# A spectral block on one core: stage two regrouped onto halves of the TensorE array

## The chip, the core and the metric

The kernel runs on one core of one Trainium2 chip. The metric is the device time of one execution in microseconds, as the median of several runs. The profile is of one execution; its times are microseconds from the start of the span unless marked ns. PE is TensorE, the matrix engine, and PEld its weight loads; DVE is VectorE, ACT ScalarE, POOL GpSimd, SP SyncE, which issues the DMAs here. L492 is line 492 of the kernel.

## The reference: what is computed

A block on 2048 rows of 512 values, in fp32: a modulation vector from `c`, a layer norm, a two-dimensional FFT filter, a gated residual, a second norm, a dense layer with Mish, and a second gated residual.

```python
mod = (_silu(c) @ w_mod).reshape(c.shape[0], 6, 1, -1)
sa, ca, ga, sb, cb, gb = (mod[:, 0], mod[:, 1], mod[:, 2], mod[:, 3], mod[:, 4], mod[:, 5])
h = _layernorm(x, axis=-1) * (1 + ca) + sa
x = x + ga * irfft2(rfft2(h) * (w_r + 1j * w_i), s=(S, D))
h = _layernorm(x, axis=-1) * (1 + cb) + sb
x = x + gb * (mish(h @ w1 + b1) @ w2)
```

The filter is the part that matters here. A transform over 2048 rows is split into one of 128 and one of 16, a transform over 512 values into one of 128 and one of 4.

## The kernel before

The kernel has four stages that follow one another on TensorE.

Stage one (to about 50 us) normalises the input and does the long parts of both transforms. It leaves `a_sb`: for each of 64 columns q a tile of 128 partitions (the row frequency within 128) by 128 numbers, 16 row remainders by 8 (four value remainders, real and imaginary).

Stage two (`p2_...`, about 50 to 99.5 us) finishes the forward transform over the 16 x 8 numbers of a column, multiplies by the filter, and starts the way back. It goes over 17 groups of columns: column 0 alone (the "zero group", with its own functions `z_...`, since it also holds the values that a real transform folds away), columns 1 to 3, and then fours. A group takes five steps:

- `p2_in`: a transpose of each column on PE (L471), one copy out of PSUM by ACT (L474), and `p2_shift`, a small sum on POOL that adds the norm's shift to one element of each column (L482);
- `p2_mul`: for each column one fp32 matmul with the column as stationary operand and the constants `kf` moving, 128 x 128 (L492). The result has the row frequency on partitions;
- `p2_prod`: two DVE products of 512 with the filter's real and imaginary part (L508), then a difference and a sum of 256 each (L513, L514) on POOL, or the difference on DVE in the first and last groups;
- `p2_back`: a second transpose of each column on PE (L525) and a copy by ACT (L528);
- `p2_out`: for each column one fp32 matmul with the column stationary and `kv` moving (L538). `store_d` copies the result out of PSUM on ACT with the two operations of L391 and L392, for each of the two halves `dd[0]` and `dd[1]`.

The order is written out by hand (`manual_schedule`). The first eight groups are brought in ahead (`LEAD`), then each step s of the loop issues, in this order, products of group s, matmuls of group s + 1, transposes of group s + 3, a step of the modulation, second transposes of group s - 2 and the way back of group s - 3. PSUM has eight banks; each kind of step has two of its own (tags A to D). SBUF buffers come in rings of two by tag.

Beside the groups the same loop computes the four parts of the modulation that later stages need: 16 weight tiles of 256 KB, fetched by SP through a ring of four (`mod_fetch`, L551), each one DVE step (`mod_late`: L115, L117, or L120 with a read of the sum). The gate of the first residual is spread over partitions by a matmul with ones and multiplied into `kiv` (`mod_gate`, L563 and L564), that of the second by `apply_gate` (L568, L569) at the end. The filter comes in 16 pieces of 256 KB, `wqa` in stage one and `wqb` at the start of stage two, in the space that stage one's input ring leaves. `kc`, two transfers of 1 MB for stage three, is issued at step 9.

Stage three (from 99.5) ends the inverse transform (L676, L677, L686), adds the residual and prepares the weights of the dense layers; its first matmul needs `dd[0]` of all columns. Stage four (from about 143) is the dense layers in three-term split precision, which take the rest.

Of the kernel before, what the change touches and what calls it, by code (L numbers as in the profile page):

```python
# [12 lines left out]
P = 128  # L13
# [18 lines left out]
def tile_spectral_block(ctx: ExitStack, tc: tile.TileContext, x_d, w1_d, b1_d, w2_d,  # L32
# [68 lines left out]
    wqa = pw.tile([P, 8, 2, 64, 4], F32, name="wqa")  # L101
# [5 lines left out]
    kv = pw.tile([P, 512], F32, name="kv")  # L107
# [83 lines left out]
    def load_rest():  # L191
        nc.sync.dma_start(kf, kf_d)
        nc.sync.dma_start(wz, wz_d)
        for i in range(8):
            nc.sync.dma_start(wqa[:, i], wq_d[i])
            if i == 2:
# [189 lines left out]
    def store_d(ps, q0, nq):  # L386
        src = ps[:, 0:nq * 128].rearrange("p (q a c) -> p a c q", q=nq, c=2)
        for i in range(2):
            dst = dd[i].rearrange("p n d c q -> p (n d) c q")
            s = src[:, 32 * i:32 * i + 32]  # L390
            nc.scalar.copy(dst[:, :, 0:2, q0:q0 + nq], s)  # L391
            nc.scalar.mul(dst[:, :, 2, q0:q0 + nq], s[:, :, 0, :], -1.0)  # L392

    groups = [(0, 1), (1, 3)] + [(q0, 4) for q0 in range(4, NQ, 4)]

    seq = [1, 2, 3, 4, 0] + list(range(5, len(groups)))
    early = [big.tile([P, 4, 512], F32, name=f"early{i}", tag=t) for i, t in enumerate(("cr", "ci"))]

    def zbuf(g):
        i = seq.index(g)  # L400
        return early[i // 4][:, i % 4] if i < 8 else buf("h")
# [13 lines left out]
    def z_in():  # L415
        ps = bank("A")
        nc.tensor.transpose(ps[:, 0:P], a_sb[:, 0, :, :].rearrange("p n e -> p (n e)"), ident)
        z = zbuf(0)
        turned(z, ps[:, 0:P])
        nc.gpsimd.tensor_tensor(z[:, 0:1], z[:, 0:1], saz[:, 0:1], op=ALU.add)  # L420
        st["z", 0] = z

    def z_mul():
        z = st.pop(("z", 0))
        pb = bank("B")
        reflected(pb[:, 0:160], z, lambda i: kf[:, 128 + 160 * i:288 + 160 * i])
        st["pb", 0] = pb

    def z_prod():
        pb = st.pop(("pb", 0))  # L430
        pbv = pb[:, 0:160].rearrange("p (c j k) -> p c j k", c=2, j=5)
        pr = []
        for i in range(2):
            t = buf(("g1", "g2")[i])
            tv = t[:, 0:160].rearrange("p (c j k) -> p c j k", c=2, j=5)
            nc.vector.tensor_tensor(tv, pbv, wz[:, i].unsqueeze(1).to_broadcast([P, 2, 5, N2]), op=ALU.mult)
            pr.append(t)
        y = buf("y")
        nc.gpsimd.tensor_tensor(y[:, 0:80], pr[0][:, 0:80], pr[1][:, 80:160], op=ALU.subtract)
        nc.gpsimd.tensor_tensor(y[:, 80:160], pr[0][:, 80:160], pr[1][:, 0:80], op=ALU.add)  # L440
        nc.gpsimd.tensor_copy(y[:, 160:256].rearrange("p (i k) -> p i k", i=3),
                              y[:, P:P + 32].unsqueeze(1).to_broadcast([P, 3, 32]))
        st["y", 0] = y

    def z_back():
        y = st.pop(("y", 0))
        pc = bank("C")
        nc.tensor.transpose(pc[:, 0:P], y[:, 0:P], ident)
        nc.tensor.transpose(pc[0:96, P:2 * P], y[:, 160:256], ident)
        t1, t2 = buf("t"), buf("t")  # L450
# [7 lines left out]
    def z_out():  # L458
        t1, t2 = st.pop(("t", 0))
        pe = bank("D")  # L460
        reflected(pe[:, 0:P], t1, lambda i: kv[:, 128 + i * P:256 + i * P], [(t2[0:96, 0:P], kw)])
        store_d(pe, 0, 1)

    def p2_in(g):
        if g == 0:
            return z_in()
        q0, nq = groups[g]
        w = nq * P
        ps = bank("A")
        for i in range(nq):  # L470
            nc.tensor.transpose(ps[:, i * P:(i + 1) * P],  # L471
                                a_sb[:, q0 + i, :, :].rearrange("p n e -> p (n e)"), ident)
        z = zbuf(g)
        nc.scalar.copy(z[:, 0:w], ps[:, 0:w])  # L474
        st["z", g] = z
        if seq.index(g) >= 2:
            p2_shift(g)

    def p2_shift(g):
        q0, nq = groups[g]  # L480
        zc = st["z", g][:, 0:nq * P:P]
        nc.gpsimd.tensor_tensor(zc, zc, saz[:, q0:q0 + nq], op=ALU.add)  # L482

    def p2_mul(g):
        if g == 0:
            return z_mul()
        q0, nq = groups[g]
        w = nq * P
        z = st.pop(("z", g))
        pb = bank("B")  # L490
        for i in range(nq):
            nc.tensor.matmul(pb[:, 0:w].rearrange("p (e q) -> p e q", q=nq)[:, :, i], z[:, i * P:(i + 1) * P],  # L492
                             kf[:, 0:128], start=True, stop=True)
        st["pb", g] = pb

    def p2_prod(g):
        if g == 0:
            return z_prod()
        q0, nq = groups[g]
        w = nq * P  # L500
        pb = st.pop(("pb", g))
        pbv = pb[:, 0:w].rearrange("p (c j q) -> p c j q", q=nq, c=2)
        pr = []
        for i in range(2):
            t = buf(("g1", "g2")[i])
            tv = t[:, 0:w].rearrange("p (c j q) -> p c j q", q=nq, c=2)
            wt = (wqa, wqb)[q0 // 32][:, q0 // 4 % 8, i, :, q0 % 4:q0 % 4 + nq]
            nc.vector.tensor_tensor(tv, pbv, wt.unsqueeze(1).to_broadcast([P, 2, 64, nq]), op=ALU.mult)  # L508
            pr.append(t)
        y = buf("y")  # L510
        u = w // 2
        eng = nc.vector if g in (*seq[:3], *seq[-2:]) else nc.gpsimd
        eng.tensor_tensor(y[:, 0:u], pr[0][:, 0:u], pr[1][:, u:w], op=ALU.subtract)  # L513
        nc.gpsimd.tensor_tensor(y[:, u:w], pr[0][:, u:w], pr[1][:, 0:u], op=ALU.add)  # L514
        st["y", g] = y

    def p2_back(g):
        if g == 0:
            return z_back()
        q0, nq = groups[g]  # L520
        w = nq * P
        y = st.pop(("y", g))
        pc = bank("C")
        for i in range(nq):
            nc.tensor.transpose(pc[:, i * P:(i + 1) * P], y[:, 0:w].rearrange("p (e q) -> p e q", q=nq)[:, :, i],  # L525
                                ident)
        t = buf("t")
        nc.scalar.copy(t[:, 0:w], pc[:, 0:w])  # L528
        st["t", g] = t

    def p2_out(g):
        if g == 0:
            return z_out()
        q0, nq = groups[g]
        t = st.pop(("t", g))
        pd = bank("D")
        for i in range(nq):
            nc.tensor.matmul(pd[:, i * P:(i + 1) * P], t[:, i * P:(i + 1) * P], kv[:, 0:128],  # L538
                             start=True, stop=True)
        store_d(pd, q0, nq)  # L540

    late = {}
    work_mod = {s: [] for s in range(len(seq) + 4)}
    when = (3, 4, 5, 6, 6, 7, 8, 9, 9, 10, 11, 12, 12, 13, 14, 16)
    for i, s in enumerate(when):
        work_mod[s].append((i // 4, i % 4))

    def mod_fetch(s):
        for which, k in work_mod.get(s, ()):
# [11 lines left out]
    def mod_gate():  # L561
        ga = bank("A")
# [3 lines left out]
    def apply_gate():  # L566
        gb = bank("B")
# [4 lines left out]
    wqb = pw.tile([P, 8, 2, 64, 4], F32, name="wqb", tag="half")  # L572
    with tc.manual_schedule():
        for i in range(8):
            nc.sync.dma_start(wqb[:, i], wq_d[8 + i])
        for i in range(LEAD):
            p2_in(seq[i])
            if i == 1:
                for g in seq[:2]:
                    p2_shift(g)  # L580
            if i in (2, 4):
                p2_mul(seq[i // 2 - 1])
            if i == 3:
                p2_prod(seq[0])
        for s in range(len(seq) + 3):
            mod_fetch(s + 2)
            if 0 < s < len(seq):
                p2_prod(seq[s])
            if 2 <= s + 1 < len(seq):
                p2_mul(seq[s + 1])  # L590
            if LEAD <= s + 3 < len(seq):
                p2_in(seq[s + 3])
            mod_late(s)
            if 2 <= s < len(seq) + 2:
                p2_back(seq[s - 2])
            if s >= 3:
                p2_out(seq[s - 3])
            if s == 7:
                mod_gate()
            if s == 14:  # L600
                plus_one(cols[:, 1, 1, :], cols[:, 1, 1, :])
            if s == 9:
# [377 lines left out]
def _constants():  # L980
# [79 lines left out]
    kv = np.concatenate([bwd(4, backward)] + [m[:128] for m in zero], 1)  # L1060
# [6 lines left out]
def _layout(x, w_r, w_i, w_mod):  # L1067
# [12 lines left out]
    wq = wq.reshape(2, 128, 4, 16, 16, 4).transpose(4, 1, 0, 2, 3, 5).reshape(16, 128, 2, 64, 4)  # L1080
# [36 lines left out]
```

## Time and profile before

| | us |
|---|---|
| median of 3 runs | 390.17 |
| lowest and highest | 389.27, 391.98 |
| profiled execution | 389.86 |
| its span | 387.8 |
| TensorE busy | 380.7 |
| VectorE busy | 298.9 |
| ScalarE busy | 247.2 |
| GpSimd busy | 96.3 |

The time of an execution is some 2 us over its span: 389.86 beside 387.8. A busy time is a union, so overlapping instructions count once. Matmuls are pipelined: the duration that a row gives for one is its latency, and the cost of one in a row of many is the distance from start to start. An fp32 matmul stands in the trace as two weight loads and two matmul records. In a merged row of the timeline the first number is the start, the second the length of the whole row, and xN the count; what stands in square brackets is the idle time ahead of it and what ended it.

### The profile page before, as it was taken

Reading aid. Unit: us, or ns where it says so; the run is one execution under the profiler, and the core shown is the slowest. Engines: PE = TensorE matmul, PEld = TensorE weight load, DVE = VectorE, ACT = ScalarE, POOL = GpSimd, SP = SyncE. Lnnn points to the kernel's source line nnn. Section 1 sums busy time; section 2 is a strip of 40 time slices with the busy share of each in tenths; the row PEclk is TensorE's granted clock in tenths of the full one; section 3 lists DMA queues with packets and bytes.
Section 4 is the critical chain, followed back from the end, with each engine's and each line's share of the span. In section 5 each row is a group of like instructions: output and inputs, shape, how many; then the busy total and the mean of one; then the engine's idle time right before and its main releaser. Section 6 shows DMA issues by size and latency. Waiting matters only on the chain.

```text
span 387.8 us, 7373 instructions
## 1 busy us (share of the span) xinstructions
PE 380.7 (98%) x2744; PEld 353.1 (91%) x2744; DVE 298.9 (77%) x668; ACT 247.2 (64%) x545; POOL 96.3 (25%) x132
## 2 busy tenths in 40 slices
PE   8999999999999999999999999999999999999996
PEld 8899789999999998998998998999999999899984
DVE  2898879777199989897866965965966875987993
ACT  1788656678459746985755664674674675584750
POOL 0677636675067543210000000000000010017000
PEclk9999999999999999999999999999999999999999
DMA  7999995481224420200100100100100200122011
GB/s 250 380 308 348 313 341 154 122 339 41 70 83 120 132 62 28 57 1 2 56 0 3 54 2 0 57 0 2 55 2 0 76 0 2 55 70 94 3 54 54
DMA packets 21316, 36.70 MB, mean 95 GB/s; under 512 B 3841, under 2 KB 6753, under 8 KB 21025
## 3 DMA queue, kind: packets, MB, share of 16 engines
q1 hardware_dynamic: 21280, 36.24, 28.2%
q8 instruction: 21, 0.34, 0.4%
q14 instruction: 15, 0.11, 0.1%
HBM read 32.04 MB, written 4.20 MB: 93 GB/s over the span
## 4 chain that ended last, share of the span: by engine, by line
PE 84%; DVE 5%; DMA 4%; ACT 4%; issue 1%; SPq 0%; DVEq 0%; ACTq 0%
PE bank L818 24%; PE bank L765 20%; PE bank L767 10%; PE bank L492 3%; PE bank L538 3%; PE bank L686 3%; PE bank L677 3%; PE bank L676 3%; PE bank L810 2%; PE bank L830 2%; DMA modr<-scb 2%; PE bank L655 2%; PE bank L471 2%; PE bank L258 2%; PE bank L525 1%
## 5 line engine op out<-in xcount | busy, mean ns | idle before, releaser
L775 ACT ACTIVATE buf<-bank,b1n 128x256 f32<-128x256 f32 (+1 forms) x88 | 40.7, 471 | 63.9 <-PE bank L767 62.7
L776 DVE TENSOR_TENSOR buf<-buf,bank 128x256 f32<-128x256 f32 (+1 forms) x88 | 35.3, 417 | 36.4 <-ACT buf L775 36.4
L728 DVE TENSOR_TENSOR al<-buf,ah 128x512 fp32r<-128x512 f32 (+2 forms) x85 | 53.8, 658 | 0.7 <-ACT ah L727 0.7
L747 POOL TENSOR_TENSOR buf<-buf,modr 128x512 f32<-128x512 f32 (+1 forms) x3 | 3.9, 1293 | 180.5 <-DVE buf L776 144.4
L765 PE MATMUL bank<-h2o,w1h 128*128 128x512 f32 (+1 forms) x176 | 47.9, 394 | 0.0
L765 PE MATMUL bank<-h2e,w1h 128*128 128x512 f32 (+1 forms) x176 | 47.9, 394 | 0.0
L727 ACT CAST ah<-buf 128x512 fp32r<-128x512 f32 (+2 forms) x85 | 43.0, 548 | 1.2 <-DVE buf L792 1.2
L792 DVE TENSOR_TENSOR buf<-buf 128x128 f32<-128x128 f32 x148 | 39.9, 311 | 3.5 <-ACT buf L782 2.2
L782 ACT ACTIVATE buf<-buf 128x512 f32<-128x512 f32 (+1 forms) x48 | 28.6, 596 | 15.8 <-DVE buf L776 15.7
L818 PE MATMUL bank<-w2a,ah 128*128 128x256 f32 x161 | 34.6, 284 | 0.0
L765 PEld LDWEIGHTS bank<-h2o,w1h 128*128 128x128 f32 (+1 forms) x176 | 29.8, 186 | 4.6 <-DVE buf L776 0.3
L765 PEld LDWEIGHTS bank<-h2e,w1h 128*128 128x128 f32 (+1 forms) x176 | 30.0, 186 | 4.2
L818 PE MATMUL bank<-w2b,ah 128*128 128x256 f32 x147 | 31.3, 279 | 0.0
L767 PEld LDWEIGHTS bank<-h2o,w1l 128*128 128x128 f32 (+1 forms) x176 | 26.8, 185 | 4.0
L767 PEld LDWEIGHTS bank<-h2e,w1l 128*128 128x128 f32 (+1 forms) x176 | 26.7, 186 | 4.0
L767 PE MATMUL bank<-h2e,w1l 128*128 128x256 f32 (+1 forms) x176 | 27.8, 280 | 0.0
L767 PE MATMUL bank<-h2o,w1l 128*128 128x256 f32 (+1 forms) x176 | 27.8, 280 | 0.0
L818 PEld LDWEIGHTS bank<-w2a,ah 128*128 128x128 f32 x161 | 26.3, 188 | 0.0
L677 PE MATMUL bank<-kc,d 128*128 128x128 f32 x128 | 24.8, 276 | 0.0
L676 PE MATMUL bank<-kc,d 128*128 128x128 f32 x128 | 24.7, 275 | 0.0
L818 PEld LDWEIGHTS bank<-w2b,ah 128*128 128x128 f32 x147 | 24.2, 188 | 0.0
L127 DVE BATCH_NORM_STATS2 st<-x 128x6 f32<-128x512 f32 x32 | 22.0, 688 | 0.4
(224 smaller groups left out, 999.2 us busy)
## 6 DMA issues: line engine op xcount, KB each, us to landing
buf<-in_B_w_dram SPq DMA_DIRECT2D x20, 256.0 KB, 2.9
x<-in_A_x_dram SPq DMA_DIRECT2D x16, 256.0 KB, 5.1
xring<-in_x_t_dram SPq DMA_DIRECT2D x16, 256.0 KB, 5.0
wm<-in_w_mod_dram SPq DMA_DIRECT2D x16, 256.0 KB, 4.4
out_dram<-x SPq DMA_DIRECT2D x7, 512.0 KB, 2.6
mraw<-in_km_dram SPq DMA_DIRECT2D x16, 128.0 KB, 4.7
wqa<-in_w_q_dram SPq DMA_DIRECT2D x8, 256.0 KB, 4.4
wqb<-in_w_q_dram SPq DMA_DIRECT2D x8, 256.0 KB, 6.1
```

The source lines that it names most:

```text
L127: nc.vector.bn_stats(t, x[:, n, :])
L676: nc.tensor.matmul(o, dj[:, 0:128], kc[0][:, n, :], start=True, stop=False)
L677: nc.tensor.matmul(o, dj[:, 64:192], kc[1][:, n, :], start=False, stop=True)
L727: nc.scalar.copy(h, r)
L728: nc.vector.tensor_tensor(l, r, plain(h), op=ALU.subtract)
L765: nc.tensor.matmul(ps, w1h[:, k, fs], h[:, k], start=(k == 0), stop=False)
L767: nc.tensor.matmul(ps[:, 0:256], w1l[:, k, fs], h[:, k, 0], start=False, stop=(k == 3))
L775: nc.scalar.activation(o, ps[:, 256:], AF.Identity, bias=b1n[:rows, f:f + 1])
L776: nc.vector.tensor_tensor(o, o, ps[:, 0:256], op=ALU.add)
L782: nc.scalar.activation(o, o, AF.Mish)
L792: nc.vector.tensor_tensor(o, p, q, op=op)
L818: nc.tensor.matmul(o, a[p][:, e], w2[t][q][:, r], start=(own and half == 0 and t == 1 and i == 0), stop=(end and i == 2 and (n, half) != ( ...
```

## The change

Stage two goes over eight pairs of groups, eight columns each, and swaps the operands of the product by `kf`.

- `p2_in` transposes whole columns of `a_sb` as before, eight a pair into two banks, and ACT copies each bank back over the columns in `a_sb` (`zs`). One `p2_shift` covers the pair.
- `p2_mul`: `kf` is the stationary operand, 64 of its columns at a time, and the four transposed columns of a group are moving, 512 wide. The two groups of a pair (h) write to the lower and upper 64 partitions of one bank, that is they use two halves of the array's columns; c picks the real or the imaginary 64 columns of `kf`. So there are four matmuls of 512 a pair where there were eight of 128. The result has the transform's lanes on partitions, 64 of each group, real and imaginary parts in two banks.
- `p2_prod`: four DVE products of 512 and a difference and a sum of 512; the difference is on POOL, the sum on POOL, or on DVE for the last two pairs. The filter's tiles are laid out on the host to match, in eight pieces of 512 KB.
- `p2_back` is gone for all but the zero group.
- `p2_out`: for each column and each c a matmul with 64 partitions of the product as stationary operand, real and imaginary part accumulating. The two groups of a pair lie on the two halves of the array's rows and write two banks. So there are 16 matmuls of 64 x 128 by 128 a pair where there were eight of 128 x 128. `kv` holds its 64 rows twice, once for each half.
- The zero group does without its own first transpose, since column 0 is transposed with its pair, and its steps are issued between those of the pairs.
- All banks come from one ring over the eight. The last pair's second stores are on DVE.
- The fetches of the modulation have a new distribution over the pairs; the first three stand between the first and second piece of `wqb` on SP's queue. `kc` is issued in iteration 3 of eight.

```diff
-    wqa = pw.tile([P, 8, 2, 64, 4], F32, name="wqa")
+    wqa = pw.tile([P, 4, 2, 512], F32, name="wqa")
...
-    kv = pw.tile([P, 512], F32, name="kv")
+    kv = pw.tile([P, 640], F32, name="kv")
...
+    def ring():
+        return bank("ABCD"[next(count) % 4])
+
+    zs = a_sb.rearrange("p q n e -> p q (n e)")
+    lanes = 64
...
+    def p2_in(p):
+        for h in range(2):
+            ps = ring()
+            for i in range(4):
+                nc.tensor.transpose(ps[:, i * P:(i + 1) * P], zs[:, 8 * p + 4 * h + i], ident)
+            nc.scalar.copy(z_of(p, h), ps)
+
+    def z_of(p, h):
+        return zs[:, 8 * p + 4 * h:8 * p + 4 * h + 4].rearrange("p q s -> p (q s)")
+
+    def p2_shift(p):
+        zc = zs[:, 8 * p:8 * p + 8, 0]
+        nc.gpsimd.tensor_tensor(zc, zc, saz[:, 8 * p:8 * p + 8], op=ALU.add)
+
+    def p2_mul(p):
+        st["pb", p] = pbs = []
+        for c in range(2):
+            pb = ring()
+            for h in range(2):
+                nc.tensor.matmul(pb[lanes * h:lanes * h + lanes], kf[:, lanes * c:lanes * c + lanes], z_of(p, h),
+                                 start=True, stop=True)
+            pbs.append(pb)
+
+    def p2_prod(p):
+        re, im = st.pop(("pb", p))
+        wr, wi = ((wqa, wqb)[p // 4][:, p % 4, i] for i in range(2))
+        t = [buf(tag) for tag in ("y", "t", "g1", "g2")]
+        st["y", p] = t[:2]
+        nc.vector.tensor_tensor(t[0], re, wr, op=ALU.mult)
+        nc.vector.tensor_tensor(t[1], re, wi, op=ALU.mult)
+        nc.vector.tensor_tensor(t[2], im, wi, op=ALU.mult)
+        nc.gpsimd.tensor_tensor(t[0], t[0], t[2], op=ALU.subtract)
+        nc.vector.tensor_tensor(t[3], im, wr, op=ALU.mult)
+        eng = nc.vector if p >= 6 else nc.gpsimd
+        eng.tensor_tensor(t[1], t[1], t[3], op=ALU.add)
+
+    def p2_out(p):
+        y = st.pop(("y", p))
+        pd = ring(), ring()
+        for i in range(4):
+            o = slice(i * P, i * P + P)
+            for c in range(2):
+                for h in range(2):
+                    if (p, h, i) != (0, 0, 0):
+                        rs = slice(lanes * h, lanes * h + lanes)
+                        nc.tensor.matmul(pd[h][:, o], y[c][rs, o], kv[rs, c * P:c * P + P],
+                                         start=(c == 0), stop=(c == 1))
+        last = p == pairs - 1
+        for i, h in ((i, h) for i in range(2) for h in range(2)):
+            nq = 3 if (p, h) == (0, 0) else 4
+            store_d(pd[h], 8 * p + 4 * h + 4 - nq, nq, i, nc.vector if last and h else None)
...
+    work_mod = [(0, 1), (1, 2), (2, 3), (3, 2), (4, 3), (5, 3), (6, 2)]
...
+        for i in range(4):
+            nc.sync.dma_start(wqb[:, i], wq_d[4 + i])
+            if i == 0:
+                mod_fetch(0)
+                mod_fetch(1)
+        for p in range(2):
+            p2_in(p)
+            p2_shift(p)
+        for p in range(pairs):
+            p2_mul(p)
+            if p == 0:
+                z_in()
+            if p + 2 < pairs:
+                p2_in(p + 2)
+            if p:
+                p2_out(p - 1)
+            if p == 1:
+                z_mul()
+            if p == 3:
+                z_back()
+            if p == 4:
+                mod_gate()
+            p2_prod(p)
+            if p == 1:
+                z_prod()
+            if p + 2 < pairs:
+                p2_shift(p + 2)
+            mod_late(p)
+            mod_fetch(p + 2)
...
+        z_out()
+        p2_out(pairs - 1)
         apply_gate()
```

More of the change, by code (lines that the diff above doesn't have):

```diff
@@ L384, in tile_spectral_block, with store_d @@
     dd = [big.tile([P, 8, 4, 3, NQ], F32, name=f"d{i}", tag=t) for i, t in enumerate(("da", "db"))]
[L386 to L390, printed above, removed]
+    def store_d(ps, q0, nq, i, eng=None):
+        src = ps[:, (4 - nq) * P:].rearrange("p (q a c) -> p a c q", q=nq, c=2)
+        dst = dd[i].rearrange("p n d c q -> p (n d) c q")
+        s = src[:, 32 * i:32 * i + 32]
+        if eng is None:
             nc.scalar.copy(dst[:, :, 0:2, q0:q0 + nq], s)
             nc.scalar.mul(dst[:, :, 2, q0:q0 + nq], s[:, :, 0, :], -1.0)
[L394 to L401, printed above, removed]
+        else:
+            eng.tensor_copy(dst[:, :, 0:2, q0:q0 + nq], s)
+            eng.tensor_scalar(dst[:, :, 2, q0:q0 + nq], s[:, :, 0, :], -1.0, None, op0=ALU.mult)
+    count = iter(range(1000))
+    def ring():
+        return bank("ABCD"[next(count) % 4])
+    zs = a_sb.rearrange("p q n e -> p q (n e)")
+    lanes = 64
     def turned(dst, src):
@@ L415, in z_in @@
     def z_in():
[L416 to L420, printed above, removed]
+        z = buf("h")
+        turned(z, zs[:, 0])
         st["z", 0] = z
@@ L446, in z_back @@
         y = st.pop(("y", 0))
-        pc = bank("C")
+        pc = ring()
         nc.tensor.transpose(pc[:, 0:P], y[:, 0:P], ident)
         nc.tensor.transpose(pc[0:96, P:2 * P], y[:, 160:256], ident)
-        t1, t2 = buf("t"), buf("t")
+        t1, t2 = buf("h"), buf("h")
         turned(t1, pc[:, 0:P])
@@ L459, in z_out @@
         t1, t2 = st.pop(("t", 0))
[L460 to L494, printed above, removed]
@@ L517, in p2_back @@
[L517 to L540, printed above, removed]
+        pe = ring()
@@ L542, in tile_spectral_block @@
+    pairs = NQ // 8
     late = {}
[L543 to L546, printed above, removed]
+    work_mod = [(0, 1), (1, 2), (2, 3), (3, 2), (4, 3), (5, 3), (6, 2)]
+    ends = [sum(n for _, n in work_mod[:i]) for i in range(len(work_mod) + 1)]
+    work_mod = [[(i // 4, i % 4) for i in range(a, b)] for a, b in zip(ends, ends[1:])] + [[]] * 3
     def mod_fetch(s):
-        for which, k in work_mod.get(s, ()):
+        for which, k in work_mod[s]:
@@ L561, in mod_gate @@
     def mod_gate():
-        ga = bank("A")
+        ga = ring()
         nc.tensor.matmul(ga, ones, modr[:, 0], start=True, stop=True)
@@ L566, in apply_gate @@
     def apply_gate():
-        gb = bank("B")
+        gb = ring()
         nc.tensor.matmul(gb, ones, modr[:, 2], start=True, stop=True)
@@ L1059, in _constants @@
     zero = [bwd(5, unlanes(r)) for r in (None, 15 - k2, (16 - k2) % 16)]
[L1060 removed]
+    both = np.tile(bwd(4, backward).reshape(2, 64, 128).swapaxes(0, 1).reshape(64, 256), (2, 1))
+    kv = np.concatenate([both] + [m[:128] for m in zero], 1)
     kw = np.concatenate([m[128:] for m in zero], 0)
```

62 lines of the change are left out of this document (10 added, 52 removed).

## The prediction

> **What bounds the kernel now.** I read the head of the page first, then the chain of waits, then the busy times of the stretch that the change rewrites.
>
> ```profile
> span 387.8 us, 7373 instructions
> PE 380.7 (98%) x2744; PEld 353.1 (91%) x2744; DVE 298.9 (77%) x668; ACT 247.2 (64%) x545; POOL 96.3 (25%) x132
> PE 84%; DVE 5%; DMA 4%; ACT 4%; issue 1%; SPq 0%; DVEq 0%; ACTq 0%
> ```
>
> TensorE (PE) is busy 98% of the span and carries 84% of the chain, so a stage is as long as its matmuls unless they wait. Stage two runs from its first product by kf at 52.38 to the first matmul of stage three at 99.51 (both rows below). The view of busy times by stretch gives that stretch and a steady part of it:
>
> ```profile
> 52.38:99.51 47.13, 46.42 (x391) 44.01 (x390) 35.39 (x68) 32.78 (x102) 27.95 (x49) 1.00 0.59 196
> 74.22:90.00 15.78, 15.78 (x143) 15.78 (x141) 13.24 (x29) 12.15 (x36) 11.88 (x18) 1.00 0.65 237
> ```
>
> The columns are the length, then PE, weight loads, VectorE (DVE), ScalarE (ACT), GpSimd (POOL), the granted clock and the DMAs. PE idles 0.7 us in 47.13, and never in the steady part; there DVE has 16% to spare. The clock is full. One step of the loop, a group of four columns, from the timeline of PE:
>
> ```profile
> 74.22 1.06 PE L538 MATMUL bank<-kv,buf 128*128 128x128 f32 x8
> 75.11 1.06 PE L492 MATMUL bank<-kf,buf 128*128 128x128 f32 x8
> 76.00 0.60 PE L471 MATMUL bank<-ident,a_sb 128*128 128x128 f32 x4
> 76.44 0.64 PE L525 MATMUL bank<-ident,buf 128*128 128x128 f32 x4
> 76.92 1.06 PE L538 MATMUL bank<-kv,buf 128*128 128x128 f32 x8
> ```
>
> Read the distances of the starts: a step is 2.70 us, so a pair of groups is 5.40. Four fp32 matmuls are eight records, each matmul two in a row, 0.89 us, 0.111 a record. Four transposes into the stage are 0.44 (0.11 each), four out of it (L525) 0.48.
>
> **The prices of the new matmuls.** Nothing in the trace runs on half an array. The nearest rows are the zero group's, with one stationary column (L410) between full ones, and the gate's 512-column matmul (PE's timeline, then that of its weight loads):
>
> ```profile
> 70.38 0.39 PE L409 MATMUL bank<-kv,buf 128*128 128x128 f32 x2
> 70.69 0.38 PE L410 MATMUL bank<-kv,buf 128*1 128x128 f32 x2
> 71.00 0.49 PE L412 MATMUL bank<-kw,buf 96*128 96x128 f32 x2
> 71.33 0.39 PE L413 MATMUL bank<-kv,buf 128*128 128x128 f32 x2
> 71.55 1.02 PE L563 MATMUL bank<-modr,ones 128*128 128x512 f32 x2
> 72.41 1.05 PE L492 MATMUL bank<-kf,buf 128*128 128x128 f32 x8
> ```
>
> ```profile
> 71.00 0.30 PEld L412 LDWEIGHTS bank<-kw,buf 96*128 96x128 f32 x2 [0.22 <-issue]
> ...
> 71.98 0.19 PEld L492 LDWEIGHTS bank<-kf,buf 128*128 128x128 f32 x1 [0.24 <-issue]
> 72.41 0.86 PEld L492 LDWEIGHTS bank<-kf,buf 128*128 128x128 f32 x7 [0.24 <-issue]
> ```
>
> A record of 512 columns takes (72.41 - 71.55)/2 = 0.43. *Product by kf*, four matmuls of 512 columns a pair: eight records, 3.44 one after another, 1.72 two at a time. I take 2.15, by the order of the records: both records of a matmul stand together and use the same half, so the first of the other half queues behind the second of this one and starts beside it. Eight records then start at 0, 1, 1, 2, 2, 3, 3, 4 units and end at 5, 5 x 0.43. *Way back*, 16 matmuls of 128 columns: 32 records, 3.57 in a row, 1.78 two at a time, by the same order 17 x 0.111 = 1.89; I take that.
>
> The Trainium skill ("TensorE: Matmul & The Clock Gate", Part 3 on packing small matmuls) reports 2.38 times the speed for three column tiles and 3.07 for four row tiles. At the same share of the ideal two halves would give some 1.6 and 1.5, an estimate: 2.2 and 2.3 in place of 2.15 and 1.89, and the sum below would be about 4 us longer. No run here shows it yet.
>
> *Change of array shape.* From 70.38 to 71.55 are eight records, 0.89 at the steady pace; they took 1.17. Going to the one column and back costs 0.28, 0.14 a change; weight loads wait there (0.22 <-issue) and are not taken ahead. The bounds are 0, if halves are not told apart from the whole, and 0.22. I take 0.14. The loop changes shape three times an iteration (into the product, into the transposes, into the way back); with the zero group, two gates and short first and last iterations I count 27.
>
> **The sum on PE**, from the first product by kf to stage three: products 8 x 2.15 = 17.2; transposes in, six pairs behind the first product, 6 x 8 x 0.11 = 5.3; way back 8 x 1.89 less the zero column = 15.0; zero group 2 x 1.17 + 2 x 0.11 = 2.6 (as before, less one transpose); the two gates 2 x 0.86 = 1.7; shapes 27 x 0.14 = 3.8. Together 45.6. The removed L525, 63 of them, 7.6 us, pay for what the halves lose in stagger and changes. In the loop a pair is 0.88 + 2.15 + 1.89 + 0.42 = 5.34 against 5.40.
>
> Where it starts and ends, from PE's timeline and the groups of ACT and POOL (behind the busy time stands the mean in ns):
>
> ```profile
> 50.82 1.72 PE L471 MATMUL bank<-ident,a_sb 128*128 128x128 f32 x11
> 52.38 0.83 PE L492 MATMUL bank<-kf,early 128*128 128x128 f32 x6
> ...
> 99.51 0.39 PE L676 MATMUL bank<-kc,d 128*128 128x128 f32 x2
> ```
>
> ```profile
> L391 ACT COPY d<-bank 128x256 f32<-128x256 f32 x30 | 11.5, 382 | 2.9 <-PE bank L538 2.9
> L528 ACT COPY buf<-bank 128x512 f32<-128x512 f32 x15 | 9.0, 602 | 2.8 <-PE bank L525 2.8
> L392 ACT ACTIVATE d<-bank 128x128 f32<-128x128 f32 x29 | 8.8, 302 | 0.0
> L474 ACT COPY buf<-bank 128x512 f32<-128x512 f32 x9 | 5.3, 590 | 3.6 <-PE bank L471 3.6
> ```
>
> ```profile
> L242 POOL TENSOR_TENSOR buf<-buf 128x512 fp32r<-128x512 f32 x7 | 9.4, 1337 | 5.8 <-ACT buf L241 5.8
> ...
> L482 POOL TENSOR_TENSOR buf<-buf,saz 128x4 f32<-128x4 f32 x9 | 3.7, 408 | 0.0
> ```
>
> The first product now needs eight columns: both copies (2 x 0.59 after the first four transposes, 51.3 to 52.5) and the shift on POOL (0.4): 52.9, 0.5 later. 52.9 + 45.6 = 98.5, 1.0 before 99.51. For waits of PE I keep 0.4 of the 0.7 there are now. So 0.6 less.
>
> **What must stay hidden.** ACT: two copies of 0.59 and four stores of 0.38 + 0.30 are 3.9 a pair, under 5.34; its L528 go. POOL: two sums of 512 columns (1.34) and a shift (0.41), 3.1 a pair. DVE:
>
> ```profile
> L508 DVE TENSOR_TENSOR buf<-bank,wqb 128x512 f32<-128x512 f32 x16 | 10.2, 679 | 0.6 <-POOL buf L514 0.6
> ...
> L120 DVE SCALAR_TENSOR_TENSOR wm<-wm,modr 128x512 f32<-128x512 f32 x8 | 6.0, 756 | 1.2 <-DMA wm<-in_w_mod_dram 1.2
> L117 DVE SCALAR_TENSOR_TENSOR modr<-wm,sc,modr 128x512 f32<-128x512 f32 x6 | 5.3, 879 | 0.0
> ```
>
> Four products at 0.68 are 2.7 a pair, as now, and up to three steps of the modulation (0.76 to 0.88) 2.5: 5.2, nearly PE's 5.34. Who waits if DVE is late: the way back of pair p-1, which PE reaches behind the transposes of p+1, the way back of p-2, the product of p and the transposes of p+2: 0.9 + 1.9 + 2.15 + 0.9 and four changes, 6.4 us after the product of p-1. Its data need four DVE products (2.7) and the tail on POOL (1.34 behind the last), 4.1. So 2.3 us of lag are covered; the gate's extra DVE step (0.7) in iteration four fits in. The last pair has only the way back of p-1 and the zero group ahead, 3.3, and its second sum is on DVE: 0 to 1 us, in the 0.4.
>
> On SP the order moves: three weight fetches pass three of wqb's four pieces, which are wanted from pair five on, 20 us later; kc's loads go behind the fetches for iteration five, which wait for ring buffers (up to 3.9 us now, an iteration then, to some 81), and stage three wants kc only at 98.5. wqa comes in pieces of 512 KB with kv behind the second; pair zero uses the first alone. If a piece were late it would cost its own landing, some 5 us, once.
>
> ```profile
> SPq L551 <- DVE wm L120: 14.1, 8, 3.9
> ```
>
> ```profile
> wqb<-in_w_q_dram SPq DMA_DIRECT2D x8, 256.0 KB, 6.1
> ```
>
> The profiled execution took 389.86, the median is 390.17. 389.86 - 0.6 = 389.3; at the median 389.6.
>
> **The rivals.** *Halves run fully side by side.* Products 13.8, way back 14.1: PE's sum falls to 41.3, stage three starts at 52.9 + 41.3 + 0.4 = 94.6, 4.9 less. Were the changes of shape free as well it would be 8.7 less, but there DVE sets the end: it is busy 35.4 us in the stretch now and keeps nearly all of it, since only its small sums go and two of 512 columns come. From the first half product on, 54.3, 35 us of work end at 89.3, and way back and gate (3.0) at 92.3, 7.2 less. So 383.0 to 385.3, mid 384.2. For it: the halves share no rows or no columns, and PE's idle share now is nil. Against it: the order of the records. Chance 0.31.
>
> *Weight loads go one at a time.* At 71.98 one load of L492 was taken ahead under the gate's second record; the next began at 72.41, as the first matmul of L492 did. If on row halves too a load starts only when the matmul before it starts, each of the 254 records of the way back waits for its own load of 128 columns, at the 0.111 of today's pace: 28.2 in place of 15.0, 13.2 more, 402.8. It decides as soon as two loads cannot run side by side, since load and matmul are of the same length here; the products by kf, 0.43 long, hide theirs. For it: every load in the trace starts so. Against it: the trace has one pair of buffers on the whole array, halves could have their own. Chance 0.21. The Trainium skill (the same page and part) says that a load is taken ahead of running matmuls where the row groups differ, which would speak against this rival; no run here has two row groups.
>
> *Halves are not concurrent at all*, the change does not do what it says: products 27.5 and way back 28.2 make 23.5 more, 413. Chance 0.07.
>
> *A lag of DVE or POOL past the cover*, by POOL's sums in each other's way with DVE: 3 to 6 us, 393 to 396. Chance 0.08.
>
> **How the numbers follow.** The forecast, halves staggered by the order of the records, has 0.33 and is good for 386 to 394: changes of shape at 0 (3.8 less) or at 0.22 (2.1 more), and loads in each other's way by a sixth of the 13.2 (2.2 more). A measurement tells 1%, 3.9 us, from no change. Faster by that: nine tenths of the first rival and a sixth of the forecast, 0.34. Slower: the load rival, the serial one, most of the lag, 0.35. Within: the rest, 0.31. The range goes from within the first rival, 383.5, to the load rival with its products a little late, 404; the serial case and the ends of the others are outside, under 0.2.
>
> **What would show it.** Records of the two halves overlapping, pairs starting together; a product of about 2.15 a pair and a way back of about 1.9. If the way back takes 3.5, loads are serial; if products take 1.7 and DVE has no idle time, the first rival. PEld idle <-issue at each change of shape, 0.1 or so, confirms the changes. A PE that waits for POOL or DVE ahead of the way back says lag. The forecast is wrong if stage three starts before 96 or after 101.

## The result and the profile after

| | before | after |
|---|---|---|
| median, us | 390.10 | 400.44 |
| lowest and highest | 389.27, 391.98 | 399.85, 401.36 |
| profiled execution | 389.86 | 401.36 |
| its span | 387.8 | 398.2 |

The change makes the kernel slower: 1.026 times the time before (95% interval 1.022 to 1.030), 10.3 us. The forecast was 389.6. The head of the page of the kernel after, and its chain of waits by engine:

```profile
span 398.2 us, 7299 instructions
...
PE 383.0 (96%) x2745; PEld 339.3 (85%) x2745; DVE 306.5 (77%) x669; ACT 237.2 (60%) x525; POOL 92.6 (23%) x110
...
PE 75%; DMA 9%; DVE 8%; ACT 3%; issue 2%; SPq 1%; POOL 1%; ACTq 0%; DVEq 0%; POOLq 0%
```

TensorE's share of the chain fell from 84% to 75%, VectorE's rose from 5% to 8% and GpSimd has appeared with 1%. The DMAs' rose as well, from 4% to 9%, on the loads of stage one (`x`, `xring`, `mraw`), but stage two starts only 0.8 later than before (53.17 beside 52.38). The stretches of stage two, by length, then the busy times of PE, weight loads, DVE, ACT and POOL, the clock and the DMAs:

```profile
53.17:109.93 56.76, 48.26 (x384) 29.33 (x385) 42.39 (x67) 22.51 (x83) 24.34 (x27) 0.91 0.41 139
62.23:67.11 4.88, 4.88 (x50) 3.21 (x49) 4.68 (x9) 1.41 (x4) 2.85 (x5) 1.00 0.37 107
72.35:85.39 13.04, 9.16 (x52) 5.21 (x51) 6.03 (x10) 5.15 (x21) 3.75 (x4) 0.74 0.19 47
```

Stage two took 47.13 and takes 56.76, 9.6 more: nearly the whole loss is here. But the second row, one steady pair, is 4.88, which is less than the 5.40 of before and than the 5.34 of the forecast. The third row, one pair and the gate, takes 13.04 at a mean clock of 0.74. So the halves are quick, and something else stops them. The timeline of PE shows both:

```profile
62.23 1.94 PE L483 MATMUL bank<-a_sb,kf 128*64 128x512 f32 x8
64.10 1.09 PE L468 MATMUL bank<-ident,a_sb 128*128 128x128 f32 x8
65.12 2.06 PE L509 MATMUL bank<-kv,buf 64*128 64x128 f32 x32
67.11 1.94 PE L483 MATMUL bank<-a_sb,kf 128*64 128x512 f32 x8
...
70.00 2.06 PE L509 MATMUL bank<-kv,buf 64*128 64x128 f32 x32
71.98 0.33 PE L447 MATMUL bank<-ident,buf 128*128 128x128 f32 x1
...
74.59 1.09 PE L468 MATMUL bank<-ident,a_sb 128*128 128x128 f32 x8
78.43 0.68 PE L509 MATMUL bank<-kv,buf 64*128 64x128 f32 x4 [2.74 <-POOL buf L495]
80.10 3.36 PE L509 MATMUL bank<-kv,buf 64*128 64x128 f32 x28 [0.99 <-POOL buf L498]
83.39 2.07 PE L537 MATMUL bank<-modr,ones 128*128 128x512 f32 x2
85.39 1.94 PE L483 MATMUL bank<-a_sb,kf 128*64 128x512 f32 x8
...
89.45 0.49 PE L509 MATMUL bank<-kv,buf 64*128 64x128 f32 x4 [1.10 <-POOL buf L495]
91.12 2.36 PE L509 MATMUL bank<-kv,buf 64*128 64x128 f32 x28 [1.18 <-POOL buf L498]
...
106.66 2.38 PE L509 MATMUL bank<-kv,buf 64*128 64x128 f32 x32 [1.46 <-POOL buf L495]
```

From start to start, a product by kf (L483) is 1.87 with one change of shape in it, the transposes (L468) 1.02, the way back (L509) 1.99. In the single records of the trace the matmuls of the two halves start 6 to 7 ns apart. From 74.59 on PE waits for POOL ahead of each way back or within it. Behind the waits the granted clock drops: it is 1.00 from 53.17 to 78.59, 0.50 to 85.42, 1.00 to 92.25, 0.50 to 95.66, and 1.00 from there to the end of the stage. So the 28 records at 80.10 take 3.36 where later ones take 1.83, and the gate's matmul 2.00 to the next start, where the experiment with both steps moved, below, has 1.06 (75.75 to 76.81). Half speed makes the stall longer. The Trainium skill ("TensorE: Matmul & The Clock Gate", Part 1) says that the clock is halved once PE has been idle for about one window of 3.4 us. These rows agree in kind only: the first drop, at 78.59, comes behind one wait of 2.74, with transposes ahead of it, and the second behind 1.10 and 1.18 with four records between them, so here less idle time was enough.

What POOL waits for is read from DVE's timeline in the same place, and from POOL's:

```profile
69.70 0.68 DVE L120 SCALAR_TENSOR_TENSOR wm<-wm,modr 128x512 f32<-128x512 f32 x1
70.32 0.08 DVE L120 DVE_READ_ACCUMULATOR wm<-wm,modr 128x1 f32 x1
74.16 0.29 DVE L407 COPY buf<-bank 128x127 f32<-128x127 f32 x1 [3.77 <-ACT buf L406]
74.83 0.28 DVE L453 COPY buf<-bank 32x127 f32<-32x127 f32 x1 [0.38 <-ACT buf L452]
75.14 0.69 DVE L492 TENSOR_TENSOR buf<-bank,wqa 128x512 f32<-128x512 f32 x1
...
77.55 1.38 DVE L120 SCALAR_TENSOR_TENSOR wm<-wm,modr 128x512 f32<-128x512 f32 x1
...
78.85 1.74 DVE L120 SCALAR_TENSOR_TENSOR wm<-wm,modr 128x512 f32<-128x512 f32 x1
80.52 0.08 DVE L120 DVE_READ_ACCUMULATOR wm<-wm,modr 128x1 f32 x1
85.50 0.69 DVE L538 TENSOR_TENSOR kiv<-kiv,bank 128x512 f32<-128x512 f32 x1 [4.90 <-PE bank L537]
86.10 0.69 DVE L492 TENSOR_TENSOR buf<-bank,wqb 128x512 f32<-128x512 f32 x1
```

```profile
77.11 1.26 POOL L495 TENSOR_TENSOR buf<-buf 128x512 f32<-128x512 f32 x1 [4.37 <-DVE buf L494]
78.33 1.71 POOL L498 TENSOR_TENSOR buf<-buf 128x512 f32<-128x512 f32 x1
```

The matmuls by kf of pair three were over at 69.0 and DVE was free at 70.40, but its four products (L492 on) start only at 75.14, 4.7 later. What stands ahead of them in DVE's queue are two small copies of `z_back`, 0.29 each, and these wait for transposes that PE does behind the way back of pair two and for ACT's stores of that way back. One pair later the same thing happens with the gate's product L538: DVE is free at 80.60 and held until 85.50, since the gate's matmul stands on PE behind the way back of pair three. And that way back waits for the products of pair three, which were late. So each hold hands its delay to the other engine.

The rows show a second thing: L120, one of the modulation's steps, takes 0.68 at 69.70, and 1.38 and 1.74 while POOL does its sums (77.11 to 80.04). Each of the two ends 0.56 or 0.55 after the sum that started before it: at 78.93 behind the difference L495, which ends at 78.37, and at 80.59 behind the sum L498, which ends at 80.04. L498 itself lies beside the first of them and takes 1.71, where L495 takes 1.26.

### The profile page after: what moved, and what is told of

The parts are those of the page before. It is cut to its first block, busy times and chain, and to the rows that moved or that the text cites. A ratio compares the mean times of both kernels' runs of the same rounds, so it can differ in the third digit from the quotient of the medians.

```text
span 398.2 us, 7299 instructions
## 1 busy us (share of the span) xinstructions
PE 383.0 (96%) x2745; PEld 339.3 (85%) x2745; DVE 306.5 (77%) x669; ACT 237.2 (60%) x525; POOL 92.6 (23%) x110
## 4 chain that ended last, share of the span: by engine, by line
PE 75%; DMA 9%; DVE 8%; ACT 3%; issue 2%; SPq 1%; POOL 1%; ACTq 0%; DVEq 0%; POOLq 0%
PE bank L797 23%; PE bank L744 19%; PE bank L746 10%; PE bank L509 3%; PE bank L665 3%; DMA x<-in_A_x_dram 3%; DMA xring<-in_x_t_dram 3%; PE bank L656 2%; PE bank L655 2%; PE bank L789 2%; DMA modr<-scb 2%; PE bank L809 2%; PE bank L483 2%; PE bank L634 2%; DMA mraw<-in_km_dram 1%
## 5 line engine op out<-in xcount | busy, mean ns | idle before, releaser
L509 PE MATMUL bank<-kv,buf 64*128 64x128 f32 x252 | 20.1, 306 | 8.4 <-POOL buf L495 5.9
L509 PEld LDWEIGHTS bank<-kv,buf 64*128 64x128 f32 x252 | 17.4, 208 | 12.4 <-POOL buf L495 8.4
L391 ACT COPY d<-bank 128x256 f32<-128x256 f32 (+2 forms) x32 | 12.3, 389 | 23.9 <-PE bank L509 23.9
L656 PE MATMUL bank<-kc,d 128*128 128x128 f32 x128 | 24.7, 275 | 0.0
```

Of the source, the lines that this page charges most:

```text
L509: nc.tensor.matmul(pd[h][:, o], y[c][rs, o], kv[rs, c * P:c * P + P], start=(c == 0), stop=(c == 1))
L656: nc.tensor.matmul(o, dj[:, 64:192], kc[1][:, n, :], start=False, stop=True)
```

## The experiments

Three theories are told apart. **Q**, the queue: two small DVE steps that wait for PE stand ahead of products that are ready. **C**, contention: DVE's steps on two SBUF operands and POOL's sums of 512 keep each other out, so that DVE has no time to spare. **H**, the order on the halves: two halves run side by side only if their matmuls stand next to each other in the queue. The times of before, taken beside each group of runs, had medians from 389.67 to 390.06; a ratio is to that median.

**Both waiting steps moved, one at a time and together.** In the loop:

```diff
-            if p == 3:
-                z_back()
-            if p == 4:
-                mod_gate()
             p2_prod(p)
...
             mod_late(p)
+            if p == 3:
+                z_back()
+            if p == 4:
+                mod_gate()
```

With only `z_back` moved:

> The zero group's way back is issued at the end of iteration 3 instead of ahead of the products of pair 3; TensorE's own order is the same. Theory Q (VectorE's queue: two small copies of the zero group that wait for TensorE and ScalarE stand ahead of the four products): in the changed kernel VectorE was free at 70.4 and the products of pair 3 began at 75.14; they begin at about 70.5, the way back of pair 3 no longer waits 2.7 and 1.0 us, and the products of pair 4, held behind the gate, begin at about 79.4 instead of 86.1. About 6.7 us off: 393.5. Theory C (VectorE and GpSimd in each other's way over SBUF make VectorE too slow, whatever the order): the lag comes back within two pairs, less than 3 us off: 397.5 or more.

With only `mod_gate` moved:

> The gate's matmul, and VectorE's multiplication that waits for it, are issued at the end of iteration 4 instead of ahead of the products of pair 4; TensorE's own order is the same. Theory Q: the products of pair 3 still begin at 75.1, those of pair 4 at about 80.6 instead of 86.1: 5.5 us off, 395. Theory C: less than 3 us off, 397.5 or more.

With both:

> Both moved. Theory Q alone (the halves are worth what the trace shows, a pair 4.9 us, and nothing else is late): stage three begins near 95 instead of 109.9, 385. Theory Q with C (the holds go, but from pair 3 on VectorE takes 5.2 to 6.4 us a pair, since its modulation steps of 0.7 us take 1.4 to 1.7 beside GpSimd's sums): products of pair 5 begin at about 84 instead of 92.2, 8 us off, 392. Theory C alone: 397 or more.

Measured were 393.62 with `z_back` moved (ratio 1.010, interval 1.006 to 1.013), 395.93 with the gate moved (1.018, 1.012 to 1.023), and 391.24 with both (1.004, 1.002 to 1.006). Of the 10.3 us, 6.8, 4.5 and 9.2 are gone. The first two together would be 11.3, more than both give: they pass delay to each other, as read above; with `z_back` alone moved, the gate still holds DVE, but for 1.75 in place of 4.90. Q is shown. PE's rows at the way back of pair three, with the gate alone moved:

```profile
78.19 0.49 PE L509 MATMUL bank<-kv,buf 64*128 64x128 f32 x4 [2.74 <-POOL buf L495]
79.86 3.36 PE L509 MATMUL bank<-kv,buf 64*128 64x128 f32 x28 [1.18 <-POOL buf L498]
83.15 1.18 PE L537 MATMUL bank<-modr,ones 128*128 128x512 f32 x2
```

and the same place with `z_back` alone moved:

```profile
75.93 2.06 PE L509 MATMUL bank<-kv,buf 64*128 64x128 f32 x32
77.92 1.12 PE L537 MATMUL bank<-modr,ones 128*128 128x512 f32 x2
```

The wait of 2.74 belongs to `z_back` alone and goes with it. But Q by itself would have brought 385, and with both moved the time is 391.2. Stage two has these busy times there, and DVE one pair like this:

```profile
51.69:99.65 47.96, 44.72 (x385) 27.49 (x385) 42.26 (x67) 22.43 (x83) 24.33 (x27) 0.96 0.47 162
```

```profile
75.21 0.69 DVE L492 TENSOR_TENSOR buf<-bank,wqb 128x512 f32<-128x512 f32 x1
...
77.61 1.46 DVE L120 SCALAR_TENSOR_TENSOR wm<-wm,modr 128x512 f32<-128x512 f32 x1
...
78.99 1.75 DVE L120 SCALAR_TENSOR_TENSOR wm<-wm,modr 128x512 f32<-128x512 f32 x1
...
80.67 0.68 DVE L120 SCALAR_TENSOR_TENSOR wm<-wm,modr 128x512 f32<-128x512 f32 x1
...
81.29 0.68 DVE L538 TENSOR_TENSOR kiv<-kiv,bank 128x512 f32<-128x512 f32 x1
81.89 0.68 DVE L492 TENSOR_TENSOR buf<-bank,wqb 128x512 f32<-128x512 f32 x1
```

From one pair's products to the next are 6.68 without a gap, against PE's 4.88 and 1.06 for the gate: DVE sets the pace. The three steps on `wm` take 1.38, 1.68 and 0.62 from start to start; the last, with no sum of 512 beside it, is under the 0.76 to 0.88 that the prediction used for all.

**Contention: fewer steps on DVE, or smaller sums on POOL.** Both are made on the version with both steps moved. In the first, 14 of the 16 steps of the modulation become a copy of one element:

```diff
-                mod_column(w, cols[:, 1, which - 1, k:k + 1], 1.0, w)
+                nc.vector.tensor_copy(cols[:, 1, which - 1, k:k + 1], w[:, 0:1])
+            elif k:
+                nc.vector.tensor_copy(modr[:, 0 if which == 0 else 2, k:k + 1], w[:, 0:1])
```

> The kernel with both steps late (391.2) with 14 of VectorE's 16 modulation steps cut to a copy of one element each: this leaves out most of the modulation vectors. Theory C (with the holds gone, VectorE's modulation steps, slowed by GpSimd's sums, set the pace from pair 3 on): stage two is TensorE's own 41 to 43 us plus the zero group's waits, about 5 us less: 386. Without C (VectorE not the limit): 390 or more.

The same edit in the kernel before, as a control:

> The kernel before the change, with the same 14 of 16 modulation steps cut to one element: this leaves out most of the modulation vectors. Theory C (VectorE's load became the limit only through the change): here TensorE has no idle time to give back, at most the 0.7 us it idles in stage two: 389.5, no change. If the time falls by 3 us or more, fewer VectorE steps help any version, and the gain of the cut steps in the changed kernel says nothing of the change.

In the other, DVE's steps stay and POOL's sums go down to four columns:

```diff
-        nc.gpsimd.tensor_tensor(t[0], t[0], t[2], op=ALU.subtract)
+        nc.gpsimd.tensor_tensor(t[0][:, 0:4], t[0][:, 0:4], t[2][:, 0:4], op=ALU.subtract)
...
-        eng.tensor_tensor(t[1], t[1], t[3], op=ALU.add)
+        w = 512 if p >= 6 else 4
+        eng.tensor_tensor(t[1][:, 0:w], t[1][:, 0:w], t[3][:, 0:w], op=ALU.add)
```

> The kernel with both steps late (391.2), in which GpSimd's difference and sum of 512 columns are cut to four columns: this leaves out most of the filter's complex product. VectorE does all its steps. Theory C in the form that GpSimd's sums hold VectorE's steps (1.36 us a column step in place of 0.76): the steps fall to about 0.7, VectorE takes 4.9 us or less a pair, and TensorE waits no more: 387. In the form that VectorE simply has too many steps: they stay above 1.2 us, or the time stays at 390 or more.

Measured were 387.12 (0.994, 0.991 to 0.997) and 386.87 (0.991, 0.988 to 0.994), 4.1 and 4.4 less than with both steps moved, and 389.12 in the control (0.997, 0.995 to 1.000). The cut is worth 0.9 us in the kernel before, between 0.2 and 2.0 by the interval, and some 4 us here. That small sums bring as much, with every DVE step in place, speaks for contention; a part of it can be the shorter tail on POOL behind the products, which this run doesn't separate. It works both ways: with the DVE steps cut, POOL's sum L498 has a mean of 1337 ns, where it is 1600 with both steps moved. The contention itself is seen in the groups of DVE, the mean in ns behind the bar: first with both steps moved, then with the small sums.

```profile
L120 DVE SCALAR_TENSOR_TENSOR wm<-wm,modr 128x512 f32<-128x512 f32 x8 | 10.6, 1361 | 0.0
...
L492 DVE TENSOR_TENSOR buf<-bank,wqb 128x512 f32<-128x512 f32 x4 | 2.7, 683 | 0.0
```

```profile
L120 DVE SCALAR_TENSOR_TENSOR wm<-wm,modr 128x512 f32<-128x512 f32 x8 | 5.2, 686 | 0.0
...
L492 DVE TENSOR_TENSOR buf<-bank,wqb 128x512 f32<-128x512 f32 x4 | 2.8, 688 | 0.1
```

L120 has two operands in SBUF and goes from 1361 to 686 when POOL's sums are gone; the products, with one operand in PSUM, don't move (683 and 688). The Trainium skill ("SBUF — State Buffer", Summary: rules for kernel authors) says that a DVE operation with two SBUF inputs and a GpSimd operation that reads SBUF never run together: the second to issue waits for the whole of the first. These rows agree, and so do the ends of the two L120 at 78.93 and 80.59 in the section above; they show which of the kernel's steps are meant.

**The order of the products.** POOL's difference needs the first and third product, so the third is moved ahead of the second, and POOL starts one product earlier:

```diff
-        nc.vector.tensor_tensor(t[1], re, wi, op=ALU.mult)
         nc.vector.tensor_tensor(t[2], im, wi, op=ALU.mult)
         nc.gpsimd.tensor_tensor(t[0], t[0], t[2], op=ALU.subtract)
+        nc.vector.tensor_tensor(t[1], re, wi, op=ALU.mult)
```

With both steps moved as well:

> Both moved, and the third product of a pair is issued second, so that GpSimd's difference starts one product (0.6 us) earlier and its sum ends earlier. Theory C: one of the two collisions of a modulation step with a GpSimd sum goes, some 0.6 us a pair in the five pairs where VectorE is the slower: 3 us less than with both moved alone. Theory Q alone: no difference from it.

Alone, on the changed kernel:

> The changed kernel with nothing moved, only the third product of a pair issued second. Theory Q: the two holds stay and TensorE and VectorE keep waiting for each other in turn; the earlier sums shorten each turn by up to 0.7 us, five turns: 397 to 399. If the order of the products were the main cause, 393 or less.

Measured were 387.68 (0.994, 0.991 to 0.996), 3.6 less than without the new order, and alone 396.09 (1.016, 1.009 to 1.022), 4.3 less than the changed kernel. The second figure is rough, since its four times go from 394.84 to 399.78, and it came out under the 397 to 399 that Q gave and above the 393 of its rival. Both holds are still there in its trace, with 4.37 and 4.04; its clock was at 0.50 for 3.41 us, not for the 10.24 of the changed kernel, and how much of the gain that is stays open. POOL's difference starts one product earlier, so its tail ends earlier, and more of its work lies beside the products, which it doesn't slow, and less beside the modulation's steps. Of the second, the group of L120 in the first of the two runs is the sign, with a mean of 1141 where it was 1361; how much each of the two brings is not separated.

```profile
L120 DVE SCALAR_TENSOR_TENSOR wm<-wm,modr 128x512 f32<-128x512 f32 x8 | 8.9, 1141 | 0.0
```

**The order on the halves.** Both runs start from the version with both steps moved and the new order. In the first, all matmuls of the way back on the lower half stand ahead of those on the upper:

```diff
-        for i in range(4):
-            o = slice(i * P, i * P + P)
-            for c in range(2):
-                for h in range(2):
+        for h in range(2):
+            for i in range(4):
+                o = slice(i * P, i * P + P)
+                for c in range(2):
```

> The kernel with both steps late and the new order of products, in which the way back issues its 16 matmuls half by half: eight on the lower rows of the array, then eight on the upper, where lower and upper took turns. The sums are the same. Theory H (two matmuls run side by side only where neighbours in the queue are on different halves): the way back of a pair takes 32 x 0.111 and a change of shape, 3.7 us in place of 1.99, 1.7 a pair over 8 pairs, less the 2 us that TensorE idles now: about 11 us more, 398. Rival (the records only look side by side, or the queue finds the other half by itself): no change, 387.7.

In the second the same is done to the product by kf, `for h` around `for c`, so that two matmuls on one half stand ahead of two on the other:

> The same for the products by kf: both matmuls of a pair's first group, then both of the second, where the two groups took turns. Theory H: of eight records of 0.43 us only the middle ones meet the other half; 2.9 to 3.6 us a pair in place of 1.87, 8 to 14 over 8 pairs, less 2 us of idle time: 394 to 400. Rival: no change, 387.7.

Measured were 395.85 (1.017, 1.011 to 1.022) for the way back, and 387.68 (0.995, 0.993 to 0.998) for the product, no change from the version that both start from. The first was expected at 398 and has two times only, 395.13 and 396.56. PE in the one and in the other:

```profile
66.13 3.50 PE L509 MATMUL bank<-kv,buf 64*128 64x128 f32 x32
69.56 1.94 PE L483 MATMUL bank<-a_sb,kf 128*64 128x512 f32 x8
```

```profile
61.07 1.94 PE L482 MATMUL bank<-a_sb,kf 128*64 128x512 f32 x8
62.95 1.09 PE L468 MATMUL bank<-ident,a_sb 128*128 128x128 f32 x8
```

With eight matmuls of one half in a row the way back takes 3.43, nearly the 3.57 of 32 records one after another; with two in a row the product keeps its 1.87. H as it was put missed the second run: they need not be neighbours. In the single records of the first run the upper half starts at 67.58, as the last three of the sixteen records on the lower half are still to start; in the second run the other half starts 13 ns after the first record, with three of the first half's four still to start. So on the row halves PE found work for the idle half three records on and no further; on the column halves no more was needed.

**All together.** The version with both steps moved and the new order still had one wait ahead of the last way back, 0.86. The modulation's steps of iteration six stand ahead of the last products; they go behind them.

```diff
-            mod_late(p)
+            if p != 6:
+                mod_late(p)
+            if p == 7:
+                mod_late(6)
```

> The kernel with both steps late and the new order, with the two modulation steps of iteration 6 issued behind the products of pair 7: VectorE has the last products 1.4 us earlier, and the 0.86 us that TensorE waits ahead of the last way back goes: 386.8. If the gate's matmul behind it then waits for the steps, no change.

Measured were 386.05 (385.19 to 387.37; ratio 0.992, 0.989 to 0.995). This version beats both kernels, by 3.6 us against the times of before taken beside it, and by 14. The wait of 0.86 is gone from its trace; the time itself is 1.6 less than without this last step, and the two intervals (0.991 to 0.996 and 0.989 to 0.995) do not tell that from nothing. Its stage two:

```profile
52.28:95.44 43.16, 42.67 (x384) 26.70 (x385) 38.27 (x67) 22.39 (x83) 24.41 (x27) 1.00 0.51 181
```

PE is busy 42.67 of 43.16, at full clock. So the loss of the changed kernel can be laid out against a stage two that PE alone sets. Its 56.76 are 13.6 more: 8.0 more of PE standing idle (8.50 against 0.49) and 5.6 more of PE being busy with the same matmuls. Of these, an estimate, 4.6 are the lower clock, half of the 9.25 us that PE is busy at 0.50; the rest is the latency that every broken row of matmuls shows once more. The change's own gain, 47.13 to 43.16, is 4.0, and 9.6 is what is left.

## Why the prediction was wrong

**The step that failed** is "what must stay hidden", in two places.

First, it priced the gate's DVE step at 0.7 and said that it "fits in", under 2.3 us of lag. The step's length was right (0.69), but it asked only how long the step runs, not what the step waits for and what is queued behind it. `z_back`'s two copies, which have the same fault, were not named at all. Both steps were held 3.8 and 4.9 with four products behind them. In the kernel before the same steps stood ahead of products too, but the way back ahead of them on PE was three groups old and its data had long been there. DVE's timeline of before has the same three steps with short holds:

```profile
66.68 1.21 DVE L120 SCALAR_TENSOR_TENSOR wm<-wm,modr 128x512 f32<-128x512 f32 x1
...
68.44 0.29 DVE L405 COPY buf<-bank 128x127 f32<-128x127 f32 x1 [0.54 <-ACT buf L404]
69.97 0.28 DVE L454 COPY buf<-bank 32x127 f32<-32x127 f32 x1 [1.24 <-ACT buf L453]
...
72.61 0.69 DVE L564 TENSOR_TENSOR kiv<-kiv,bank 128x512 f32<-128x512 f32 x1 [0.43 <-PE bank L563]
```

In the changed kernel it is that of the pair before, whose data come out of the very queue that is held. This was to be read from the order of the loop and from the change's diff, without any price that was unknown. Moving the two steps took back 9.2 of the 10.3.

Second, it priced the modulation's steps by the means of before, 0.76 to 0.88, and found 5.2 us of DVE work in a pair of 5.34. Beside sums of 512 on POOL they are up to 1.38 and 1.75, and DVE had 6.7 in a pair of 5.9. The contention was in the rows of before: a group with a mean of 756 whose undisturbed length is 0.68 holds members of 1.2 (the first row above). The prediction saw that as a rival, at 0.08 and 3 to 6 us. The mechanism was right, the size fits what it costs alone (4.1 to 4.4), and the chance was too low; with the held queue on top it came to 10.3, which no rival had.

**Halves staggered by the order of the records**, the forecast's base, was wrong. Both records of a matmul stand together, but PE starts the other half's record 7 ns later and does not queue it behind the second record of the first. Products take 1.72 and 0.15, not 2.15 and 0.14, the way back 1.78 and 0.21, not 1.89 and 0.14. The estimate by the Trainium skill ("TensorE: Matmul & The Clock Gate", Part 3), 2.2 and 2.3 for the two, was too dear as well: here two halves gave twice the pace of as many records one after another, 1.78 in place of 3.57 by the 0.111 a record of before.

**The change of shape**, 0.14 by the zero group's rows, held: 0.15, 0.14 and 0.21 in the three places of a pair, 0.50 where 0.42 was counted.

**The first rival** had PE right: fully side by side, with stage two ending 41.7 after it starts. With every hold out of the way it is 43.16. Of the 1.5 more, the changes of shape in the loop are 0.6 and the zero group 0.3 (1.30 and 1.37 where 1.17 was taken twice); the rest was not taken apart. It gave 383.0 to 385.3 with DVE as the next bound, and the version that frees DVE has 386.05. It was wrong for the kernel as it stands, since it too took DVE's work as a sum of lengths: 35 us of it were to end at 89.3, while the order of the queue kept DVE idle for 3.8 and 4.9 in the middle.

**Weight loads one at a time** did not happen: a way back of 1.99 holds the loads of both halves. Its 402.8 came near the result by accident. Halves not concurrent at all is excluded by the same rows.

**The signs of being wrong** did their work: stage three started at 109.93, far after the 101 that was named, and PE waiting for POOL ahead of the way back was named as the sign of lag. The range, 383.5 to 404, held the time by luck: its upper end came from weight loads one at a time.

## What to carry to other kernels

For every small step on an engine with a queue in order, ask what it waits for and which ready work stands behind it, above all when a change shortens the distance between a product and its use: two copies of 0.3 us kept four ready products waiting for 4.7 here. Price an engine's work with the neighbours that it will have, not with means of another mix: a DVE step with two operands in SBUF was 0.68 alone and up to 1.75 beside a sum on GpSimd. Two halves of the array are worth having if their matmuls alternate; in twos they were as good on the column halves, in eights on the row halves the gain was nearly gone, and nothing between was run.

## What the runs showed that had not been expected

- Two halves of the array take fp32 records at twice the pace of one after another, on column halves (1.72 in place of 3.44 for the product) and on row halves (1.78 in place of 3.57), each half's records 6 to 7 ns behind the other's; but with eight matmuls of one half in a row nearly all of that is lost (3.43).
- A stall of PE costs more than its length: behind a wait of 2.74 the clock was at 0.50 for 6.83 us, and the waits and the lower clock of stage two stand at 8.0 and some 4.6 us, the second an estimate.
- A change of the order of two products, with nothing added or removed, was worth 3.6 us with both steps moved, and roughly 4.3 alone.
